# Ending a unit's attention one iteration later instead of four in the first 17 units, and lifting the FFN ration in the last four

## The chip, the cores and the metric

One core of one Trainium2 chip runs the kernel in one launch. The metric is device time in microseconds (us); lower is better. Five engines work side by side, each through its own queue in program order: TensorE (PE in the profile; PEld is its weight load), VectorE (DVE), ScalarE (ACT), GpSimd (POOL) and SyncE (SP, which issues most DMAs).

## The reference

Two stages, all in float32. First an attention that keeps, for every query, only the 32 largest scores of a row; then a gated feed-forward block (SwiGLU) on its output.

```python
scores = scale * np.matmul(q, k.transpose(0, 1, 3, 2))        # 8 batches, 8 heads, 576 x 576
kth = np.partition(scores, -32, axis=-1)[..., -32:-31]
scores = np.where(scores >= kth, scores, -1e9)
attn = softmax(scores)                                         # over the last axis
x = (attn @ v)  -> (B, H, S, D) to (B*S, H*D) = (4608, 512)
g = x @ w_gate                                                 # w_gate, w_val: 512 x 1536
out = (g * sigmoid(g) * (x @ w_val)) @ w_out                   # w_out: 1536 x 512
```

## The kernel before

**Units.** The attention is cut into 160 units: per batch (8), per query tile `qt` of 128 rows (0 to 3, and a rest of 64 rows as `qt` 4), per pair of heads (4). In a unit with `qt` 0 to 3 the two heads lie side by side, 1152 score columns on 128 partitions. With `qt` 4 the two heads' 64 rows share the partitions, so the unit has one head's width (`nh` = 1) and half the work on VectorE. Units 16 to 19 are the first of that kind.

A unit goes through these steps, each on its engine:

- `scores` (L220): four matmuls on TensorE (L250; L236 in a `qt` 4 unit), copied from PSUM to `sc` by ScalarE (L255, L241).
- `select` (L258): the top-k on VectorE, four rounds of `max` (L271) with three of `match_replace` (L275) between, 14 steps for two heads, then a penalty for what lies under the 32nd value (L281).
- `penalize` (L285): GpSimd adds penalty and scores (L293).
- `weigh` (L296): ScalarE's exponential with the row sum (L302).
- `normalize` (L308): GpSimd adds a small constant to the sum (L312), VectorE takes the reciprocal (L314), ScalarE scales (L317).
- `turn` (L319): nine transposes on TensorE (L329), copied out by ScalarE (L330).
- `values` (L340): the product with v on TensorE (L349, L358), copied by ScalarE into a column block `xT` of the FFN's input (L373). `finish_unit` (L507) calls it.

**FFN.** It works on 18 blocks of 256 rows. A block can start when `values` has been issued for all its rows and all four head pairs. The generator `feed` (L398) issues a block in 36 pieces: 24 of four 256-column matmuls (L412; gate and value products by turns, two pieces each) and 12 of two 512-column matmuls with `w_out` (L449). After a gate product ScalarE runs three instructions (L430 to L432) and GpSimd multiplies (L433); after a value product ScalarE copies (L437) and GpSimd multiplies (L438). These follow-ups are queued in `on_act` and `on_pool` and issued where the code calls `flush`, or in `piece` (L471) when more than one waits.

**Weights.** Each of the 72 parts of the FFN weights is loaded and rounded by a chain (`rounded`, L92): a DMA, two ScalarE instructions (L101, L106), GpSimd (L103), VectorE (L110), GpSimd (L113), VectorE (L116). `weights` staggers these, so that a rounding step issues L116, L110 with L113, L101 with L103 and L106, and a DMA, each for another part. Steps are spread between the top-k steps of `dve` (L532), 5 for every 11. Before it issues a matmul, `feed` calls `need` (L147), which issues as many rounding steps at once as are still missing.

**Order.** One loop (L524) writes out the order: iteration n holds the top-k of unit n, the scores of unit n+1, `penalize` and `weigh` of unit n-1, and in between the steps that end older units. The first half of `normalize` (L312) and what follows is for unit n-2, `turn` for n-3 (`TURN`), `values` for n-4 (`VALUES`). At the end of the function every engine is bound to this order, so an engine runs its instructions strictly as written.

**Ration.** `credit` grows by 4.6 in an iteration with two heads and 2.3 with one, to at most 8; a piece costs 1 (`pieces`, L498). It is not raised after unit 159. What is left at the end of the loop is issued without a ration (L576).

Of the kernel before, what the change touches and what calls it, by code (L numbers as in the profile page):

```python
# [27 lines left out]
def kernel(  # L28
# [33 lines left out]
    NHP = H // 2  # L62
# [80 lines left out]
    def rounding(n):  # L143
        for _ in range(n):
            next(weight, None)
# [28 lines left out]
    def load_v(i):  # L174
        b, hp = pairs[i]
        h = slice(2 * hp, 2 * hp + 2)
        vt = slabs.tile([P, 2, J, D], FP32, tag="v", name="v")
        v_last = slabs.tile([R, 2, D], FP32, tag="vl", name="v_last")
        vl = vlast[i % NV]
        nc.sync.dma_start(  # L180
            vt[:].rearrange("p h j d -> p h (j d)"),
            v[b, h, 0:JP].rearrange("h (p j) d -> p h (j d)", j=J),
        )
        nc.sync.dma_start(v_last[:], v[b, h, JP:S].rearrange("h p d -> p h d"))
        for hh in range(2):
            o = hh * R
            nc.sync.dma_start(vl[o : o + R, o : o + R], v[b, 2 * hp + hh, JP:S])
        vs[i] = (vt, v_last, vl)
# [27 lines left out]
    def n_heads(qt):  # L216

        return 1 if qt == J else 2
# [39 lines left out]
    def select(n):  # L258

        nh = n_heads(units[n][1])  # L260
        sc = state[n]["sc"]
        m = small.tile([P, 2, TOP_K], FP32, tag="m", name="m", bufs=2)
        heads = [slice(t * S, (t + 1) * S) for t in range(nh)]
        rest = work.tile([P, 2 * S], FP32, tag="rest", name="rest", bufs=1)
        e = work.tile([P, 2 * S], FP32, tag="e", name="e", bufs=4)
        state[n] |= dict(m=m, e=e, heads=heads)
        cur = sc
        rounds = TOP_K // 8
        for r in range(rounds):
            for t, hs in enumerate(heads):  # L270
                nc.vector.max(m[:, t, 8 * r : 8 * r + 8], cur[:, hs])  # L271
                yield
            if r < rounds - 1:
                for t, hs in enumerate(heads):
                    nc.vector.match_replace(  # L275
                        rest[:, hs], m[:, t, 8 * r : 8 * r + 8], cur[:, hs], LOWEST
                    )
                    yield
                cur = rest
        for t, hs in enumerate(heads):  # L280
            nc.vector.tensor_scalar(  # L281
                e[:, hs], sc[:, hs], m[:, t, TOP_K - 1 : TOP_K], FAR, ALU.is_lt, ALU.mult
            )
# [24 lines left out]
    def normalize(n):  # L308
        st = state[n]
        tot, e, heads = st.pop("tot"), st["e"], st.pop("heads")  # L310
        nh = len(heads)
        nc.gpsimd.tensor_scalar_add(tot[:, 0:nh], tot[:, 0:nh], EPS)  # L312
        yield
        nc.vector.reciprocal(tot[:, 0:nh], tot[:, 0:nh])  # L314
        yield
        for t, hs in enumerate(heads):
            nc.scalar.mul(e[:, hs], e[:, hs], tot[:, t : t + 1])  # L317

    def turn(n):  # L319

        last = units[n][1] == J
        e = state[n].pop("e")
        et = work.tile([P, 2 * J + 1, P], FP32, tag="et", name="et")
        for c0, cn in ((0, J), (J, 1)) if last else ((0, J), (J, 1), (J + 1, J)):
            ps = ps_t.tile([P, 512], FP32, tag="t", name="etps")
            kl = R if last and c0 == J else P
            for c in range(cn):
                k0 = (c0 + c) * P
                nc.tensor.transpose(ps[0:kl, c * P : (c + 1) * P], e[:, k0 : k0 + kl], ident[:])  # L329
            nc.scalar.copy(  # L330
                et[0:kl, c0 : c0 + cn, :],
                ps[0:kl, 0 : cn * P].rearrange("p (c j) -> p c j", c=cn),
            )
            if c0 == J:
                yield
        state[n]["et"] = et
# [3 lines left out]
    def values(n):  # L340

        b, qt, hp = units[n]
        vt, v_last, vl = vs[b * NHP + hp]
        et = state.pop(n)["et"]
        last = qt == J
        ql = R if last else P
        av = ps_t.tile([P, P], FP32, tag="t", name="av")
        if not last:
            nc.tensor.matmul(av[:], vl[:], et[:, J, :], start=True, stop=False)  # L349
        for c in range(J + 1 if last else J):  # L350
            kl = R if c == J else P
            for hh in range(2):
                moving = (
                    et[0:kl, c, hh * R : (hh + 1) * R]
                    if last
                    else et[:, c + hh * (J + 1), :]
                )
                nc.tensor.matmul(  # L358
                    av[hh * R : (hh + 1) * R, 0:ql],
                    v_last[:, hh, :] if c == J else vt[:, hh, c, :],  # L360
                    moving,
                    start=last and c == 0,
                    stop=c == (J if last else J - 1),
                )
        c0 = b * S + qt * P
        at = c0
        while at < c0 + ql:
            kb = at // BLK
            n_c = min((kb + 1) * BLK, c0 + ql) - at
            if kb not in xT:  # L370
                xT[kb] = ffn.tile([P, NHP, BLK], FP32, tag="xT", name="xT", bufs=3)
                done[kb] = 0
            nc.scalar.copy(  # L373
                xT[kb][:, hp, at - kb * BLK : at - kb * BLK + n_c],
                av[:, at - c0 : at - c0 + n_c],
            )
            done[kb] += n_c
            at += n_c
# [88 lines left out]
    NU = len(units)  # L467
# [3 lines left out]
    def piece():  # L471

        if len(on_act) > 1:
            flush(on_act)
        if len(on_pool) > 1:
            flush(on_pool)
        while True:
            if not current:
                if not todo or done.get(todo[0], 0) < NHP * BLK:
                    return False  # L480
                flush(on_act)
                flush(on_pool)
                current.append(feed(todo.pop(0)))
            if next(current[0], 0) == 0:
                current.pop()
                continue
            return True

    def fetch(n):

        b, qt, hp = units[n]
        i = b * NHP + hp
        if qt == 0:
            yield from prep(i)
        if qt == J and i + NHP < len(pairs):
            load(i + NHP)

    def pieces(n):  # L498
        for _ in range(n):
            if credit[0] >= 1 and piece():  # L500
                credit[0] -= 1

    def run(steps):
        for _ in steps:
            pass

    def finish_unit(n):  # L507
        values(n)
        b, qt, hp = units[n]
        if qt == J and b + 1 < B:  # L510
            load_v((b + 1) * NHP + hp)
# [7 lines left out]
    credit = [0.0]  # L519
    no = iter(())  # L520
    over = {}
    TURN, VALUES = 3, 4
    due = [0.0]
    for n in range(NU + VALUES):  # L524
        nh = n_heads(units[n][1]) if n < NU else 1
        topk = select(n) if n < NU else no
        over[n - 1] = normalize(n - 1) if 0 <= n - 1 < NU else no
        nxt = scores(n + 1) if n + 1 < NU else no
        ahead = fetch(n + 2) if n + 2 < NU else no
        norm = over.pop(n - 2, no)  # L530

        def dve(k, beside=True):  # L532

            for _ in range(k * nh):
                next(topk, None)
                due[0] += 5 / 11 if beside else 0
                if due[0] >= 1:
                    due[0] -= 1
                    rounding(1)

        if n < NU:
            credit[0] = min(credit[0] + (4.6 if nh == 2 else 2.3), 8.0)
        flush(on_act)
        next(norm, None)
        if 0 <= n - 1 < NU:
            penalize(n - 1)
        flush(on_pool)
        if 0 <= n - TURN < NU:
            run(turn(n - TURN))
        if n >= VALUES:  # L550
            finish_unit(n - VALUES)
        next(nxt, None)
        if 0 <= n - 1 < NU:
            weigh(n - 1)
        run(nxt)

        dve(2, beside=False)
        if 2 <= n + 2 < NHP:
            load(n + 2)
        if n < NHP:  # L560
            load_v(n)
        pieces(2)
        flush(on_act)
        flush(on_pool)
        dve(2)
        next(norm, None)
        run(norm)
        next(ahead, None)
        pieces(1)
        next(ahead, None)  # L570
        dve(1)
        pieces(1)
        dve(2)
        run(topk)
        pieces(6)
    while piece():  # L576
# [49 lines left out]
```

## Time and profile before

| | |
|---|---|
| time, median of 3 runs | 1922.34 us (1921.83 to 1926.45) |
| the profiled execution | 1924.16 us, span 1922.4 us |
| TensorE busy | 1759.7 us (92%) |
| VectorE busy | 1608.6 us (84%) |
| ScalarE busy | 1156.6 us (60%) |
| GpSimd busy | 815.5 us (42%) |
| mean granted TensorE clock | 0.958 |

The span is the time of one execution between its first and last recorded instruction. Busy shares are means over stages that have different limits, so the stages are to be read one by one. A row of a timeline gives start, duration, engine, line, operation, output and inputs, and in brackets the idle time before it with the instruction that ended it. The first top-k instruction of unit n starts at 138.05 us for n = 9, 166.72 for 11, 252.95 for 16, 281.55 for 20, 334.97 for 25 and 403.40 for 31.

### The profile page before, as it was taken

The page shows a single profiled execution, that of the slowest core. Times are in us where ns is not written, and L with a number is a line of the kernel's source. Part 1 is how long each engine was busy: PE and PEld are TensorE (multiplying, and loading weights), DVE is VectorE, ACT ScalarE, POOL GpSimd, SP SyncE. Part 2 cuts the span into 40 slices and gives each one's busy share as a digit, 9 for nine tenths or more (in the row PEclk, how much of TensorE's full clock was granted, in tenths as well). Part 3 has the DMA queues.
Part 4 walks back from the last instruction along what each step waited for, and adds up shares of the span by engine and source line. Part 5 has one row for each costly group of instructions (what it writes and reads, how often), then busy time and mean ns, then how long its engine had stood idle before and what let it go on. Part 6 is the DMA issues. An engine that isn't in the chain of part 4 may idle for free.

```text
span 1922.4 us, 29365 instructions
## 1 busy us (share of the span) xinstructions
PE 1759.7 (92%) x10144; PEld 1299.6 (68%) x10144; DVE 1608.6 (84%) x3476; ACT 1156.6 (60%) x2821; POOL 815.5 (42%) x846
## 2 busy tenths in 40 slices
PE   3437789989999999999999999999999999999899
PEld 2326558677777777676767776767676767686666
DVE  7999889998899979997899979998899979997300
ACT  5666666566666666665666666666666656665411
POOL 4556634434354434343434343435253525353222
PEclk7668899989999999999999999999999999999899
DMA  7222212000300011000210002000200011000000
GB/s 186 88 80 77 66 27 63 11 2 2 81 7 12 7 35 49 12 6 8 58 30 1 12 16 73 1 12 2 67 22 12 1 27 38 12 1 12 1 11 11
DMA packets 111253, 59.58 MB, mean 31 GB/s; under 512 B 89088, under 2 KB 97280, under 8 KB 111104
## 3 DMA queue, kind: packets, MB, share of 16 engines
q1 hardware_dynamic: 109904, 57.41, 11.3%
q8 instruction: 80, 1.31, 0.3%
q14 instruction: 69, 0.57, 0.1%
q10 hardware_dynamic: 1200, 0.30, 0.1%
HBM read 48.23 MB, written 9.44 MB: 30 GB/s over the span
## 4 chain that ended last, share of the span: by engine, by line
PE 82%; DVE 6%; POOL 5%; ACT 5%; issue 2%; DMA 0%; SPq 0%; POOLq 0%; DVEq 0%; ACTq 0%
PE f L412 38%; PE o_ps L449 19%; PE av L358 7%; PE etps L329 7%; PE s L250 6%; DVE m L271 3%; POOL e L293 2%; DVE rest L275 2%; PE s L236 2%; PE av L349 1%; ACT e L302 1%; PE kqps L205 1%; ACT sc L255 1%; POOL size L113 1%; POOL size L103 1%
## 5 line engine op out<-in xcount | busy, mean ns | idle before, releaser
L271 DVE MAX8 m<-rest 128x8 f32<-128x576 f32 x864 | 615.3, 747 | 2.2
L275 DVE MATCH_REPLACE8 rest<-m,rest 128x576 f32<-128x576 f32 x576 | 424.2, 743 | 0.0
L412 PE MATMUL f<-xT,wg 128*128 128x256 f32 x1728 | 407.5, 386 | 0.0
L293 POOL TENSOR_TENSOR e<-e,sc 128x1152 f32<-128x1152 f32 (+1 forms) x160 | 382.6, 2391 | 44.4 <-DVE e L281 38.4
L412 PE MATMUL f<-xT,wv 128*128 128x256 f32 x1728 | 397.3, 382 | 0.0
L449 PE MATMUL o_ps<-wo,h 128*128 128x512 f32 x864 | 387.2, 598 | 0.0
L412 PEld LDWEIGHTS f<-xT,wg 128*128 128x128 f32 x1728 | 323.9, 191 | 71.7 <-issue 30.4
L412 PEld LDWEIGHTS f<-xT,wv 128*128 128x128 f32 x1728 | 326.3, 191 | 54.4 <-issue 11.3
L433 POOL TENSOR_TENSOR h<-h,half_g 128x512 f32<-128x512 f32 x108 | 138.4, 1281 | 473.3 <-ACT h L432 455.3
L329 PE MATMUL etps<-ident,e 128*128 128x128 f32 (+1 forms) x1312 | 188.4, 288 | 130.9 <-POOL size L103 46.3
L271 DVE MAX8 m<-sc 128x8 f32<-128x576 f32 x288 | 205.6, 751 | 120.7 <-ACT sc L255 77.9
L449 PEld LDWEIGHTS o_ps<-wo,h 128*128 128x128 f32 x864 | 159.6, 190 | 192.9 <-issue 186.8
L329 PEld LDWEIGHTS etps<-ident,e 128*128 128x128 f32 (+1 forms) x1312 | 159.1, 147 | 181.6 <-issue 54.7
L330 ACT COPY et<-etps 128x512 f32<-128x512 f32 (+1 forms) x448 | 184.9, 481 | 147.4 <-PE etps L329 145.8
L302 ACT ACTIVATE e<-e,bias 128x576 f32<-128x576 f32 x288 | 222.0, 776 | 73.9 <-POOL e L293 73.5
L317 ACT ACTIVATE e<-e,tot 128x576 f32<-128x576 f32 x288 | 210.4, 780 | 5.4 <-DVE tot L314 5.1
L275 DVE MATCH_REPLACE8 rest<-m,sc 128x576 f32<-128x576 f32 x288 | 211.9, 742 | 0.0
L438 POOL TENSOR_TENSOR h<-h,val 128x512 f32<-128x512 f32 x108 | 139.6, 1292 | 161.3 <-ACT val L437 161.3
L250 PE MATMUL s<-kqT 64*128 64x288 f32 x1024 | 174.4, 449 | 10.2 <-ACT kqT L210 6.4
L358 PE MATMUL av<-et,v 128*64 128x128 f32 (+1 forms) x2560 | 175.2, 283 | 0.0
L255 ACT COPY sc<-s 128x288 f32<-128x288 f32 x512 | 165.0, 410 | 2.5 <-PE s L250 2.5
L312 POOL TENSOR_SCALAR tot<-tot 128x2 f32<-128x2 f32 (+1 forms) x160 | 37.0, 231 | 305.2 <-ACT e L302 296.5
(44 smaller groups left out, 1436.5 us busy)
## 6 DMA issues: line engine op xcount, KB each, us to landing
kq_in<-in_k_dram SPq DMA_DIRECT2D x64, 128.0 KB, 2.8
v<-in_v_dram SPq DMA_DIRECT2D x32, 256.0 KB, 3.0
kq_in<-in_q_dram SPq DMA_DIRECT2D x62, 128.0 KB, 2.9
w<-in_moe_w_gate_dram SPq DMA_DIRECT2D x24, 256.0 KB, 2.7
w<-in_moe_w_val_dram SPq DMA_DIRECT2D x24, 256.0 KB, 2.7
w<-in_moe_w_out_dram SPq DMA_DIRECT2D x24, 256.0 KB, 2.5
out_dram<-o SPq DMA_DIRECT2D x40, 128.0 KB, 2.4
out_dram<-o SPq DMA_DIRECT2D x16, 256.0 KB, 2.3
```

The source lines that it names most:

```text
L250: nc.tensor.matmul(ps[:, 0:half], slab[d, q0 : q0 + P], slab[d, k0 : k0 + half])
L255: nc.scalar.copy(sc[:, i * half : (i + 1) * half], ps[:, 0:half])
L271: nc.vector.max(m[:, t, 8 * r : 8 * r + 8], cur[:, hs])
L275: nc.vector.match_replace(rest[:, hs], m[:, t, 8 * r : 8 * r + 8], cur[:, hs], LOWEST)
L293: nc.gpsimd.tensor_tensor(e[:, every], e[:, every], sc[:, every], ALU.add)
L302: nc.scalar.activation(e[:, hs], e[:, hs], AF.Exp, bias=bias[:, t : t + 1], scale=scale, accum_out=tot[:, t : t + 1],)
L317: nc.scalar.mul(e[:, hs], e[:, hs], tot[:, t : t + 1])
L329: nc.tensor.transpose(ps[0:kl, c * P : (c + 1) * P], e[:, k0 : k0 + kl], ident[:])
L330: nc.scalar.copy(et[0:kl, c0 : c0 + cn, :], ps[0:kl, 0 : cn * P].rearrange("p (c j) -> p c j", c=cn),)
L358: nc.tensor.matmul(av[hh * R : (hh + 1) * R, 0:ql], v_last[:, hh, :] if c == J else vt[:, hh, c, :], moving, start=last and c == 0, stop=c ...
L412: nc.tensor.matmul(ps[:, i, :], w[:, kc, m * P : (m + 1) * P], x[:, kc, :], start=(kc == 0), stop=(kc == KC - 1),)
L449: nc.tensor.matmul(ps[:], hs[m // 2][:, m % 2, t * P : (t + 1) * P], wo[:, m, :], start=(m == 0), stop=(m == MC - 1),)
```

## The change

Iterations 0 to 16 (`head`) end a unit sooner: the whole of `normalize`, `turn` and `values` for unit n-1 are issued in iteration n, in the course of its top-k steps, instead of in iterations n+1 to n+3. From iteration 17 on the order is as before, and iterations 17 to 19 issue no `values` (17 and 18 no `turn`), since these units are done. The ration in the head is the same as elsewhere. From iteration 156 on the credit is set to 8 in every iteration, which also holds in the four iterations after the last unit.

```diff
+    HEAD = 4 * NHP + 1
     TURN, VALUES = 3, 4
     due = [0.0]
     for n in range(NU + VALUES):
+        head = n < HEAD
...
-        norm = over.pop(n - 2, no)
+        norm = over.pop(n - 1 if head else n - 2, no)
...
-        if n < NU:
+        if n >= NU - NHP:
+            credit[0] = 8.0
+        else:
             credit[0] = min(credit[0] + (4.6 if nh == 2 else 2.3), 8.0)
         flush(on_act)
-        next(norm, None)
+        if not head:
+            next(norm, None)
         if 0 <= n - 1 < NU:
             penalize(n - 1)
         flush(on_pool)
-        if 0 <= n - TURN < NU:
+        if HEAD - 1 <= n - TURN < NU:
             run(turn(n - TURN))
-        if n >= VALUES:
+        if n - VALUES >= HEAD - 1:
             finish_unit(n - VALUES)
...
         pieces(2)
         flush(on_act)
         flush(on_pool)
-        dve(2)
+        dve(1)
+        if head:
+            next(norm, None)
+        dve(1)
         next(norm, None)
         run(norm)
         next(ahead, None)
         pieces(1)
         next(ahead, None)
         dve(1)
         pieces(1)
+        if head and n >= 1:
+            run(turn(n - 1))
         dve(2)
+        if head and n >= 1:
+            pieces(1)
+            finish_unit(n - 1)
         run(topk)
         pieces(6)
```

## The prediction

> **What bounds the kernel now.** I read the page's slices first, then the busy time of each engine by stage, then the VectorE, ScalarE, GpSimd and TensorE timelines around the FFN's start and at the end. Times are us from the span's start. T(n), the start of iteration n, is the start of unit n's first L271 `m<-sc` on VectorE. A piece is one step of `feed`; an iteration issues what the loop body of the same n issues. "About what a measurement of this kernel can tell from no change" is 0.3%, 5.8 us.
>
> The stages (span; PE, PEld, DVE, ACT, POOL busy; PE clock) are units 11 to 15, 16 to 19, 20 to 30, 31 to 155, and the end:
>
> ```profile
> 166.72:252.95 86.23, 72.85 (x379) 56.95 (x376) 71.18 (x160) 53.79 (x132) 54.17 (x70) 0.92 0.17 55
> 252.95:281.50 28.55, 25.30 (x144) 14.01 (x141) 24.62 (x50) 16.13 (x41) 10.39 (x14) 1.00 0.11 30
> 281.50:403.40 121.90, 113.75 (x684) 83.81 (x684) 116.79 (x254) 78.44 (x194) 47.77 (x45) 0.95 0.13 33
> 403.40:1764.20 1360.80, 1337.17 (x7906) 989.42 (x7903) 1223.34 (x2612) 860.63 (x2092) 570.69 (x541) 1.00 0.09 22
> 1764.20:1922.40 158.20, 144.21 (x680) 104.28 (x678) 24.78 (x51) 49.00 (x103) 41.16 (x40) 0.95 0.03 7
> ```
>
> From unit 31 on TensorE is the bound (1337 of 1361 us). Up to unit 31 VectorE sets the pace: 117 of 122 us in units 20 to 30, where a two-head unit takes 10.57 us undisturbed. Before unit 16 it also rounds weights, about 4.5 steps (L116 and L110, 0.6 us together) per unit, and a unit takes 14.1 us. In units 11 to 15, the first with FFN work, it is idle 15 us of 86, for this reason (VectorE, then GpSimd):
>
> ```profile
> 177.16 0.29 DVE L110 TENSOR_SCALAR size<-size 128x256 int32<-128x256 int32 x1 [3.22 <-POOL size L103]
> 174.67 1.28 POOL L433 TENSOR_TENSOR h<-h,half_g 128x512 f32<-128x512 f32 x1 [4.42 <-ACT h L432]
> 194.26 0.72 POOL L113 TENSOR_TENSOR size<-size,ulps 128x256 int32<-128x256 int32 x1
> 195.06 0.40 POOL L103 TENSOR_SCALAR size<-size 128x256 f32<-128x256 f32 x1
> 195.94 0.72 POOL L113 TENSOR_TENSOR size<-size,ulps 128x256 int32<-128x256 int32 x1 [0.48 <-DVE tot L314]
> ```
>
> The queues are in order. The rounding's L103 stands on GpSimd behind an FFN product L433, that waits for ScalarE, that waits for TensorE, and VectorE waits for L103. Where VectorE has nothing else between, one rounding step follows the other after 1.68 us (194.26 to 195.94).
>
> **What moves in number.** By the code's credits (8 at most, 4.6 or 2.3 a unit) FFN block 0 has its input in iteration 8 instead of 11, block 1 in 16 instead of 19. Block 2 needs units 16 to 27, that end late in both, so it starts in iteration 31 in both. Counted through the loop, both kernels have issued 72 pieces by then and hold 8 credits; from there to iteration 155 the order is the same. So the early start wins no FFN work on TensorE: what counts is T(31), 403.4 now, and it carries over in full to the TensorE-bound stretch.
>
> **The head, iteration by iteration.** Now `normalize`'s L312 (GpSimd) stands at the start of an iteration, for a unit one older; afterwards it stands mid-iteration behind one rounding step, for unit n-1, and the reciprocal L314 on VectorE waits for it the same iteration. Queued behind L314 are the remaining 6 to 8 top-k steps and every rounding step. `turn` and `values` follow on TensorE, their PSUM copies on ScalarE.
>
> Iterations 1 to 8, no FFN: after T, L293 ends at 3.0, the exponentials at 4.7, the score copies at 5.7, L103 at 6.7, L312 at 7.0. VectorE comes to L314 between 6.1 and 7.0 (172.81-166.72 unstalled, 159.61-152.62 with its L103 wait). Cost 0.3 each, 2.4 (0 to 6); T(9) = 138.1+2.4 = 140.5.
>
> Iteration 9: six pieces are issued at the end of 8, behind `values(7)`, at T(8)+14 (transposes end at 10.1, copies at 10.9, av 2.6, xT copy 0.4). A piece is 1.72 (20.60 us for twelve at 1835.21; 3.45 for two), so they end at T(9)+10.5. GpSimd's L433 and L438 of these stand ahead of `penalize(8)`, and ScalarE's second gate (L430 to L432, 1.5 us) ahead of unit 8's exponentials. So exponentials end at 14.1, score copies at 15.3, the next value copy (two pieces later) at 16.5, L438 at 17.8, L113, L103 and L312 at 19.2. VectorE arrives at 6.8 and waits some 12 us, on L103 or L312; 7.1 us of work are left, and a cold restart of TensorE can add 1.9 (a piece took 3.78 for 1.89 at 220.06). I take 27.5 (24 to 30).
>
> Iterations 10 to 12: a gate's L433 ends at 8.9, L103 at 10.0, L312 at 10.3; VectorE arrives at 6 to 7. Lengths 17.3, 16.4, 17.3, together 51 (48 to 56); units 11 to 15 now take 16.3, 19.8, 16.3, 18.0, 15.9.
>
> Iteration 13: pieces 27 to 30 ask for the last of `w_out`, so some twelve rounding steps are issued, six and three of them with no top-k between. Each such step takes 1.68 on the L113-L103-L110 circle, VectorE being busy 0.6: 9 x 1.1 idle, plus 2 for the first, behind the score copies. 10.6 + 12 x 0.6 + 9.9 + 2 = 29.7; I take 29.2 (24 to 33). Iterations 14 and 15 have no rounding left: 10.7 each, 21.4 (21 to 24). T(16) = 140.5+27.5+51+29.2+21.4 = 269.6, now 253.0: +16.6.
>
> A rule and a row on the burst. L116 took 2.45 us at 186.44, not 0.41, ending 0.3 us after a GpSimd L293. The Trainium skill ("SBUF — State Buffer", Who interferes with whom) says that a VectorE instruction with two SBUF inputs and a GpSimd one that reads SBUF lock each other out for the whole instruction, and L116 has two. By it each burst step could lose another 0.41, so an estimate for the nine is 3.7 us more; by the 1.68 us row, none. The sum goes by the row.
>
> Iterations 16 to 19: block 1 becomes ready in 16, again with six pieces at the end of the iteration, and `scores(18)` stands behind them on TensorE. After T(16): scale at 6.7, av at 10.3, pieces 10.7 to 21.1, scores at 22.2, a gate (1.5) and exponential (0.9) ahead of the copies, which end at 24.2. VectorE is through units 16 and 17 at 14.5 and waits 10 us. Units 18, 19 and the wait for unit 20's scores: T(20) = T(16)+38 (33 to 41), now 28.6: +9.4. Units 20 to 24: as now, 53.4 (53 to 57). Units 25 to 30 carry no FFN now, as 28 to 30 before: 63.4+1 (63.4 to 68.4), now 68.4: -4. T(31) = 269.6+38+53.4+64.4 = 425.4, +22.
>
> **The end.** Here TensorE waits for a VectorE-GpSimd-ScalarE chain with its FFN pieces held back by credit:
>
> ```profile
> 1782.41 1.38 PE L329 MATMUL etps<-ident,e 128*128 128x128 f32 x9 [2.40 <-issue]
> 1791.20 1.38 PE L329 MATMUL etps<-ident,e 128*128 128x128 f32 x9 [1.40 <-issue]
> 1800.95 0.87 PE L329 MATMUL etps<-ident,e 128*128 128x128 f32 x5 [2.35 <-ACT e L317]
> 1813.80 0.77 PE L329 MATMUL etps<-ident,e 128*128 128x128 f32 x5 [2.46 <-ACT e L317]
> 1816.58 1.33 PE L329 MATMUL etps<-ident,e 128*128 128x128 f32 x5 [0.99 <-ACT e L317]
> 1820.76 3.78 PE L412 MATMUL f<-xT,wg 128*128 128x256 f32 x8
> ```
>
> From 1758.92 TensorE has 72 pieces left, 72 x 1.72 = 123.9, and attention: three units at 3.44 (1772.84 to 1776.28), one at 2.0, then 4.8 and 1.1, 18.2 in all. That is 142.1; it takes 159.1 (to 1918.0). 17 us are waits and the slow clock after them. Without rationing, iterations 156 to 158 issue 8 pieces each and 159 four, TensorE runs on to about 1833, and VectorE's chain (unit 159 scored near 1812, scaled by 1825) is done before it. What stays is the last chain, `turn(159)`, copy, `values(159)`, xT copy, with no piece to cover it, block 17 needing unit 159: 4.5 with its cold piece, taken from 1813.8 to 1822. Gain 12.5 (9 to 15). If the pieces stalled on ScalarE or GpSimd that cover would go; at 1758.92 eight ran in 13.9 us without a wait.
>
> **Sum.** +22-12.5 = +9.5 on the profiled 1924.16 (span 1922.4, 1.8 around it): 1933.7. The median lies 1.8 below that execution, so 1931.8, say 1932.
>
> **Rivals.** *The end decides, faster:* if the six late pieces do not hold up VectorE (holes of 12 and 10 us, in 9 and 16) and little else is lost, the head is near zero and 12.5 stay: 1910 to 1916. For it: TensorE idles 9.1, 7.3 and 7.4 us before L329 at 133.0, 146.8 and 160.7, so there is room for early pieces. Against: the in-order queues of ScalarE and GpSimd. It decides once the head loses under 6.7 us; 0.16.
>
> *The two halves cancel:* one of the three holes (9, 13, 16) is half as deep and the end gives its full 15: head 7 to 18, time 1917 to 1928; 0.22. *The early start changes nothing by count* holds for pieces (72 in both), and is part of all cases.
>
> *The burst and the lock cost more:* rounding circles of 2.1 us, and units 20 to 24 at their upper bound: head 30 to 36, 1940 to 1946; 0.15. The forecast's own case has 0.47, range 1928 to 1940.
>
> **How the numbers follow.** Slower by over 5.8 (above 1928.1): the forecast's case and the burst's, 0.47 + 0.15 = 0.62; same 0.22; faster 0.16. The terms' bounds, taken as independent (root of the squares), give 9 below and 10 above in the head and 3 at the end. From 1916 to 1945 the range takes in all cases but the faster one, 0.16, and the last microsecond of the burst's.
>
> **What would show it.** VectorE waiting over 10 us in iteration 9 on L103 or L312; nine L110 with waits near 1.1 in 13; an `m<-sc` wait near 10 us at unit 18 for L241; T(31) near 425; TensorE without waits from then-155's pieces to the last chain, span from T(156) 12.5 us shorter. T(31) under 410 would make the prediction wrong, as would an end as long as now.

## The result, and the profile after

The changed kernel takes 1934.60 us (median of 4 runs, 1934.09 to 1934.88), the kernel before 1922.19 us on the same chip (median of 4 runs, 1921.83 to 1926.45). The ratio is 1.0058, with a 95% interval of 1.0043 to 1.0073: 0.6% slower. The profiled execution took 1934.38 us with a span of 1932.6, 10.2 more than the span of before. The medians lie 12.4 apart, but the kernel before scatters more than the changed one: in the larger sets of runs beside the experiments its median was 1924.61 us (21 runs) and 1924.25 us (17 runs). The forecast was 1932.0, range 1916 to 1945, slower. One of the four runs of the experiment e9_act below went at a granted TensorE clock of 0.635 and took 3116.72 us, and the time given for it is that of the other three.

The 17 iterations of the head end 16 units early, units 0 to 15; unit 16 is ended as before.

The table by stage of the kernel after, cut at the starts of units 9, 11, 16, 20, 31 and 156 (span; PE, PEld, DVE, ACT, POOL busy with counts; PE clock, DMA share, GB/s):

```profile
139.38:183.17 43.79, 39.49 (x208) 32.58 (x209) 27.48 (x67) 26.09 (x64) 26.93 (x33) 0.96 0.18 57
183.17:268.01 84.84, 63.92 (x279) 36.27 (x277) 69.06 (x161) 47.42 (x119) 46.74 (x63) 0.82 0.19 62
268.01:306.80 38.79, 33.47 (x175) 26.39 (x172) 24.18 (x49) 18.50 (x45) 14.37 (x15) 0.91 0.08 18
306.80:424.52 117.72, 95.72 (x577) 69.83 (x577) 116.62 (x253) 72.57 (x182) 42.14 (x42) 0.88 0.12 30
424.52:1785.32 1360.80, 1337.20 (x7907) 989.39 (x7904) 1223.53 (x2612) 859.91 (x2092) 569.21 (x541) 1.00 0.09 22
1785.32:1932.60 147.28, 140.19 (x680) 102.32 (x678) 24.91 (x51) 48.35 (x103) 41.00 (x40) 0.97 0.03 8
```

Units 31 to 155 take 1360.80 us in both kernels, to the hundredth, with the same TensorE work. So the head is handed over in full, and the whole change stands in two numbers: T(31) is 424.52 instead of 403.40 (+21.1), and the end takes 147.28 instead of 158.20 (-10.9). In iterations 9 and 10 VectorE is busy for 27.5 of 43.8 us. Iterations 16 to 19 take 38.8 us for 24.2 of VectorE work, where before they took 28.6 for 24.6.

The VectorE timeline of after has the stalls of iterations 9, 10, 13 and 18 (in brackets the idle time, and what ended it):

```profile
158.10 0.29 DVE L110 TENSOR_SCALAR size<-size 128x256 int32<-128x256 int32 x1 [12.95 <-POOL size L103]
175.66 0.29 DVE L110 TENSOR_SCALAR size<-size 128x256 int32<-128x256 int32 x1 [3.25 <-POOL size L103]
...
225.51 0.29 DVE L110 TENSOR_SCALAR size<-size 128x256 int32<-128x256 int32 x1 [0.98 <-POOL size L103]
227.11 0.29 DVE L110 TENSOR_SCALAR size<-size 128x256 int32<-128x256 int32 x1 [0.98 <-POOL size L103]
...
292.90 0.76 DVE L271 MAX8 m<-sc 128x8 f32<-128x576 f32 x1 [10.68 <-POOL h L433]
```

Why VectorE stood for 12.95 us is read from GpSimd's timeline up to the same moment:

```profile
144.85 1.42 POOL L433 TENSOR_TENSOR h<-h,half_g 128x512 f32<-128x512 f32 x1 [6.33 <-ACT h L432]
147.35 1.26 POOL L438 TENSOR_TENSOR h<-h,val 128x512 f32<-128x512 f32 x1 [1.08 <-ACT val L437]
148.68 0.22 POOL L291 TENSOR_SCALAR bias<-m 128x2 f32<-128x2 f32 x1
148.86 2.62 POOL L293 TENSOR_TENSOR e<-e,sc 128x1152 f32<-128x1152 f32 x1
151.76 1.27 POOL L433 TENSOR_TENSOR h<-h,half_g 128x512 f32<-128x512 f32 x1 [0.27 <-ACT h L432]
155.63 1.28 POOL L438 TENSOR_TENSOR h<-h,val 128x512 f32<-128x512 f32 x1 [2.60 <-ACT val L437]
156.85 0.73 POOL L113 TENSOR_TENSOR size<-size,ulps 128x256 int32<-128x256 int32 x1
157.67 0.40 POOL L103 TENSOR_SCALAR size<-size 128x256 f32<-128x256 f32 x1
```

GpSimd takes its instructions in the order in which they were issued. Four products of the first FFN pieces stand ahead of the rounding step that VectorE waits for, and `penalize` (L293) stands between them. VectorE stands from 145.15 on; in this time GpSimd works for most of it and waits some 4.0 us (1.08, 0.27, 2.60) for ScalarE, which waits for the pieces on TensorE.

The wait of 10.68 at unit 18 is put down to L433, which L271 doesn't read. L271 reads `sc`, and the chain that leads to `sc` runs over TensorE and ScalarE: six late pieces (the three rows of L412), then the scores of unit 18, then, behind a gate and an exponential, the copy into `sc`:

```profile
278.66 4.25 PE L412 MATMUL f<-xT,wg 128*128 128x256 f32 x16
282.75 3.62 PE L412 MATMUL f<-xT,wv 128*128 128x256 f32 x16
286.20 3.62 PE L412 MATMUL f<-xT,wg 128*128 128x256 f32 x16
289.75 1.19 PE L236 MATMUL s<-kqT 64*64 64x288 f32 x8
...
292.11 0.69 ACT L241 COPY sc<-s 128x288 f32<-128x288 f32 x2
```

At the end TensorE, over the whole of iterations 156 to 159 and what follows, has two waits left. The clock granted to it was 0.50 from 1860.14 to 1866.97 and 1.00 in the stretch up to there, so the pieces behind the waits start slowly:

```profile
1858.13 0.77 PE L329 MATMUL etps<-ident,e 128*128 128x128 f32 x5 [1.74 <-ACT e L317]
1860.76 1.33 PE L329 MATMUL etps<-ident,e 128*128 128x128 f32 x5 [0.99 <-ACT e L317]
...
1864.94 4.70 PE L412 MATMUL f<-xT,wg 128*128 128x256 f32 x16
```

### The profile page after: what moved, and what is told of

It is laid out like the page before. It is cut to its first block, busy times and chain, and to the rows that moved or that the text cites. A ratio compares the mean times of both kernels' runs of the same rounds, so it can differ in the third digit from the quotient of the medians.

```text
span 1932.6 us, 29394 instructions
## 1 busy us (share of the span) xinstructions
PE 1769.6 (92%) x10144; PEld 1302.4 (67%) x10144; DVE 1607.1 (83%) x3476; ACT 1156.2 (60%) x2821; POOL 815.0 (42%) x846
## 4 chain that ended last, share of the span: by engine, by line
PE 81%; DVE 7%; ACT 5%; POOL 4%; issue 3%; DMA 0%; SPq 0%; POOLq 0%; DVEq 0%; ACTq 0%
PE f L412 38%; PE o_ps L449 18%; PE av L358 7%; PE etps L329 7%; PE s L250 6%; DVE m L271 3%; DVE rest L275 3%; POOL e L293 2%; PE s L236 2%; PE av L349 1%; ACT e L302 1%; PE kqps L205 1%; POOL size L113 1%; ACT sc L255 1%; POOL size L103 1%
## 5 line engine op out<-in xcount | busy, mean ns | idle before, releaser
L271 DVE MAX8 m<-rest 128x8 f32<-128x576 f32 x864 | 614.6, 746 | 2.2
L293 POOL TENSOR_TENSOR e<-e,sc 128x1152 f32<-128x1152 f32 (+1 forms) x160 | 382.5, 2391 | 67.0 <-DVE e L281 43.9
L449 PE MATMUL o_ps<-wo,h 128*128 128x512 f32 x864 | 396.6, 608 | 12.1 <-DVE wo L116 12.1
L412 PE MATMUL f<-xT,wg 128*128 128x256 f32 x1728 | 406.3, 385 | 0.0
L412 PE MATMUL f<-xT,wv 128*128 128x256 f32 x1728 | 396.7, 381 | 0.0
L412 PEld LDWEIGHTS f<-xT,wg 128*128 128x128 f32 x1728 | 323.8, 191 | 69.9 <-issue 27.8
L412 PEld LDWEIGHTS f<-xT,wv 128*128 128x128 f32 x1728 | 324.7, 190 | 54.3 <-issue 11.5
L433 POOL TENSOR_TENSOR h<-h,half_g 128x512 f32<-128x512 f32 x108 | 138.4, 1281 | 456.8 <-ACT h L432 438.8
L271 DVE MAX8 m<-sc 128x8 f32<-128x576 f32 x288 | 205.5, 750 | 125.8 <-ACT sc L255 71.3
L302 ACT ACTIVATE e<-e,bias 128x576 f32<-128x576 f32 x288 | 221.9, 776 | 66.2 <-POOL e L293 65.7
L317 ACT ACTIVATE e<-e,tot 128x576 f32<-128x576 f32 x288 | 210.4, 779 | 10.6 <-DVE tot L314 10.2
L438 POOL TENSOR_TENSOR h<-h,val 128x512 f32<-128x512 f32 x108 | 139.4, 1291 | 158.8 <-ACT val L437 158.7
L250 PE MATMUL s<-kqT 64*128 64x288 f32 x1024 | 167.5, 443 | 4.6 <-ACT kqT L210 4.4
L312 POOL TENSOR_SCALAR tot<-tot 128x2 f32<-128x2 f32 (+1 forms) x160 | 36.9, 230 | 318.9 <-ACT e L302 310.6
```

Of the source, the lines that this page charges most:

```text
L250: nc.tensor.matmul(ps[:, 0:half], slab[d, q0 : q0 + P], slab[d, k0 : k0 + half])
L293: nc.gpsimd.tensor_tensor(e[:, every], e[:, every], sc[:, every], ALU.add)
L302: nc.scalar.activation(e[:, hs], e[:, hs], AF.Exp, bias=bias[:, t : t + 1], scale=scale, accum_out=tot[:, t : t + 1],)
L412: nc.tensor.matmul(ps[:, i, :], w[:, kc, m * P : (m + 1) * P], x[:, kc, :], start=(kc == 0), stop=(kc == KC - 1),)
L449: nc.tensor.matmul(ps[:], hs[m // 2][:, m % 2, t * P : (t + 1) * P], wo[:, m, :], start=(m == 0), stop=(m == MC - 1),)
```

## The experiments

The **theory** is that of the prediction: the late pieces of the early FFN blocks stand, with their follow-ups, ahead of `scores`, `penalize` and the rounding chain (holes in 9 and 18); the shortened run-up makes a burst of rounding (13); the end gains by itself. **Rivals:** (a) it is not the pieces but the early end itself, L312 and L314 in the middle of the top-k, that delays VectorE; (b) the two halves act on each other; (c) the burst costs as much as the holes. The starts of units vary between executions: e1_tail issues the same as the kernel before up to iteration 155, yet its T(31) is 2.3 us later, mostly by a wait of 2.17 us ahead of unit 19 that the other execution does not have. Differences of T(31) below that are not read. The end stretch is the time from T(156) to the end of the span. The ratios are to runs of the kernel before on the same chip, each with its 95% interval.

**e1_tail and e2_head: the halves alone.** e1_tail is the kernel before with the new credit at the end; e2_head is the changed kernel with the old credit.

```diff
 e1_tail, against before
-        if n < NU:
+        if n >= NU - NHP:
+            credit[0] = 8.0
+        else:
 e2_head, against after
-        if n >= NU - NHP:
-            credit[0] = 8.0
-        else:
+        if n < NU:
```

> The ration is lifted from iteration 156 on, the head is left as in the kernel before. My theory (the two halves are separate and add): the head keeps T(31) = 403.4, TensorE runs through the end with one last chain of waits; the stretch from T(156) to the end of the span is near the changed kernel's 147.3 instead of 158.2, so the median is 1922.2 - 10.9 = 1911 (1909 to 1913). Rival (the end is shorter only because the head pushes VectorE and TensorE into another phase): 1917 to 1922. Rival (the ration at the end does nothing, TensorE's waits only move): 1922.

> The early end of units 0 to 16 alone, the ration of the end as in the kernel before. My theory: T(31) near 424.5 as in the changed kernel, the end near 158, median 1922.2 + 21 = 1943 (1941 to 1946). Rival (the head's loss is partly given back by 155, so that the two halves do not add): 1930 to 1938.

e1_tail: 1913.69 us (6 runs), ratio 0.9945 (0.9932 to 0.9957), end stretch 147.3. The end is as expected; the time is just above its range, which was counted from 1922.2, and is 10.9 under the 1924.61 of the larger set of before. e2_head: 1944.44 us (4 runs), ratio 1.0106 (1.0093 to 1.0119), T(31) 424.04, end stretch 158.15. Each end stretch is that of the kernel with the same credit to 0.1 us, and T(31) of e2_head is that of the change to 0.5. The halves add; rival (b) falls. (The later runs with a credit of 8 have end stretches of 147.2 to 149.0.)

**e3_late and e4_round: the holes and the burst.** e3_late issues no piece at the close of iterations 8 and 16; e4_round rounds 6 steps for 11 top-k steps instead of 5.

```diff
 e3_late, against after
-        pieces(6)
+        if n not in (8, 16):
+            pieces(6)
 e4_round, against after
-                due[0] += 5 / 11 if beside else 0
+                due[0] += 6 / 11 if beside else 0
```

> The changed kernel without the pieces at the very end of iterations 8 and 16, which are then issued from the next iteration on. My theory (two of the three holes come from these late pieces, that stand ahead of unit 8's and unit 16's chains and of unit 18's scores): VectorE's wait of 12.95 in iteration 9 falls under 4, that of 10.68 at unit 18 under 5, though the pieces that follow later cost some 3 to 5 each; T(31) near 411 (407 to 417), median 1934.6 - 13 = 1921 (1917 to 1927). Rival (the wait of iteration 9 belongs to the early normalize itself, not to the pieces): the 12.95 stays above 9 and the time within 4 of 1934.6.

> The changed kernel with weight rounding spread at 6 steps for 11 top-k steps instead of 5, so that iteration 13 asks for no step in a row. My theory (the third hole is the burst): the run of 0.98 to 1.9 waits on L103 in iteration 13 goes, iteration 13 takes 17 to 20 instead of 30 while iterations 1 to 12 take 0.6 longer each for the work moved there; T(16) near 259 (256 to 264), median 1934.6 - 9 = 1926 (1922 to 1930). Rival (the burst only holds work that has to be done anyway, and the denser rounding waits as long on GpSimd spread out): within 3 of 1934.6.

e3_late: 1927.19 us (10 runs), 1.0009 (1.0000 to 1.0018), T(31) 417.17. Its VectorE timeline, iterations 9 and 10:

```profile
149.70 0.29 DVE L110 TENSOR_SCALAR size<-size 128x256 int32<-128x256 int32 x1 [3.98 <-POOL size L103]
172.53 0.29 DVE L110 TENSOR_SCALAR size<-size 128x256 int32<-128x256 int32 x1 [6.61 <-POOL size L103]
```

The wait of 12.95 is down to 3.98 and the one at unit 18 is gone, so the late pieces made both. But iteration 10 now waits 6.61 instead of 3.25, and the burst moved to iteration 14 (22.5 us). T(31) gained 7.4 us where 13 were expected, and the time lies just above the expected range: the six pieces come later, and cost there.

e4_round: 1928.20 us (8 runs), 1.0020 (1.0011 to 1.0030), T(31) 416.75. Iteration 13 takes 12.3 us instead of 30.0; 9.2 of that gain are paid back as T(9) is 148.6 instead of 139.4, for the added steps run with the top-k of units 1 to 8. That is 1.15 us an iteration where 0.6 was expected, but iteration 13 also became shorter than expected, and the time lies in the expected range. Spreading the burst is thus worth about 8 us net; rival (c) is right in that holes and burst are alike in size.

**e7_both: the two together.**

> The changed kernel with both edits of e3_late and e4_round: no pieces at the end of iterations 8 and 16, rounding at 6 for 11. My theory: the burst is gone and the waits of 9 and 18 are small, but pieces that follow at the end of 9 and in 17 still cost as in e3_late; T(31) near 413 (409 to 416), median 1924 (1920 to 1927), still 10 above the tail alone. Rival (the holes were all of the loss): T(31) near 403 and median 1913.

1927.36 us (10 runs, 1918.70 to 1929.43), 1.0001 (0.9986 to 1.0015), T(31) 415.09. T(31) is as expected, the time just above its range. The two cures do not add (7.4 and 7.8 of T(31) alone, 9.4 together). What is left shows in its trace as waits of 3.64, 6.62, 4.18 and 4.11 us on L103 in iterations 9 to 12, in which the early FFN pieces run.

**e5_wait: the early end without early FFN.** `piece` starts block 0 in iteration 11 and block 1 in 19 at the earliest, as the kernel before did; all else is the change.

```diff
+                if n < {0: 11, 1: 19}.get(todo[0], 0):
+                    return False
                 flush(on_act)
```

> The changed kernel, early end of units included, but FFN block 0 may not start before iteration 11 nor block 1 before 19, as in the kernel before. My theory (the early end alone costs VectorE 0.2 to 0.3 an iteration, and the loss comes from FFN pieces that start early and late in their iteration): T(11) near 168, waits of 3 to 7 in 11 to 15 (three pieces still stand at the end of 11), no run of waits on L103 in iteration 13, no wait near 10 at unit 18; T(31) near 410 (405 to 413) instead of 424.5, median near 1924.6 + 7 - 10.9 = 1920.5 (1916 to 1924). Rival (the loss belongs to the early normalize, turn and values, whatever the FFN does): T(31) above 418, median above 1928.

1912.36 us (4 runs), 0.9935 (0.9922 to 0.9949), T(31) 401.99, both 8 us below the expectation and outside its range. Units 11 to 15, 16 to 19 and 20 to 30 of this kernel, in the columns of the stages above:

```profile
168.20:256.03 87.83, 71.59 (x351) 55.05 (x351) 71.11 (x159) 53.07 (x130) 54.25 (x69) 0.88 0.18 55
256.03:282.66 26.63, 26.42 (x127) 13.46 (x127) 24.52 (x50) 14.94 (x37) 10.05 (x13) 1.00 0.14 36
282.66:401.99 119.33, 112.00 (x682) 83.63 (x680) 116.44 (x255) 77.35 (x192) 48.14 (x45) 0.95 0.12 32
```

The burst doesn't come (FFN starts when it used to), nor do the holes, and units 16 to 30 are 4.5 us shorter than before: VectorE's waits for score copies (2.90, 0.53, 1.72, 1.33 and 1.49 before units 20 to 30) are down to 1.32 and 1.50. A likely cause is that no `turn` and `values` are left for iterations 17 and 18; that was not tried by itself. So rival (a) falls: T(31) is 1.4 us under that of before and 3.7 under e1_tail's, so ending a unit early costs nothing on balance. The loss in the head, 22.5 us of T(31) against the changed kernel, belongs to the FFN work that it lets in early.

**e6_pool: GpSimd's follow-up behind the rounding step.** In e1_tail the waits on L103 in units 11 to 15 are 3.21, 2.88, 2.68, 3.47 and 2.79, 15.0 in all, and the prediction had laid them to an L433 ahead of L103. Here GpSimd's follow-ups are issued behind it:

```diff
         flush(on_act)
-        flush(on_pool)
+        if n > 4 * NHP:
+            flush(on_pool)
         dve(2)
+        flush(on_pool)
```

> The kernel before with the ration lifted at the end (as e1_tail), and in iterations 0 to 16 the GpSimd follow-ups of the FFN (L433, L438) issued behind the rounding steps of the next four top-k steps instead of ahead of them. My theory (what costs in iterations 11 to 15 is L433 standing ahead of L103): the five waits of L110 on L103, 3.2, 2.9, 2.7, 3.5 and 2.8, shrink to under 1 each, T(16) near 241 instead of 252.7, T(31) near 393, median 1913.7 - 11 = 1903 (1899 to 1908). Rival (the wait only moves to the next rounding step, that now stands behind the same product): within 4 of 1913.7.

1911.89 us (6 runs), 0.9928 (0.9916 to 0.9940); T(16) 249.07, T(31) 401.86. A miss: the time is only 1.8 us under that of e1_tail, inside the 4 us that were named for the rival, and the intervals of the two ratios overlap. The waits shrank to 1.59, 1.17, 1.03, 1.83 and 1.15, 6.8 in all, not to under 1 each. Of these 8.2 us less, 4.4 came through: units 11 to 15 take 81.8 us instead of 86.2, for VectorE is busy for 75.0 us in them instead of 71.1. GpSimd's and VectorE's timelines in iterations 11 and 12 show both what is left of the waits and something new:

```profile
175.66 0.40 POOL L103 TENSOR_SCALAR size<-size 128x256 f32<-128x256 f32 x1 [2.06 <-ACT size L101]
176.03 1.27 POOL L433 TENSOR_TENSOR h<-h,half_g 128x512 f32<-128x512 f32 x1
```

```profile
176.10 1.35 DVE L110 TENSOR_SCALAR size<-size 128x256 int32<-128x256 int32 x1 [1.59 <-POOL size L103]
193.79 0.29 DVE L110 TENSOR_SCALAR size<-size 128x256 int32<-128x256 int32 x1 [1.17 <-POOL size L103]
```

L103 now waits for ScalarE's L101, which stands behind the gate (L430 to L432, to 175.2) on ScalarE. And L110 takes 1.35 instead of 0.29, beside the L433 that was moved there: part of the wait came back as longer VectorE instructions.

**e8_six, e9_act and e10_best: what that points to.** e8_six is e6_pool with 6.0 for 8.0 as the credit of the end, so that pieces are left for the last chain. e9_act moves ScalarE's follow-ups behind the same point as GpSimd's. e10_best is e5_wait with the credit of 6.0 and both follow-ups behind `normalize` in the head. e11_act_again is e9_act once more, for its trace.

```diff
 e8_six, against e6_pool
-            credit[0] = 8.0
+            credit[0] = 6.0
 e9_act, against e8_six
-        flush(on_act)
         if n > 4 * NHP:
+            flush(on_act)
             flush(on_pool)
         dve(2)
+        flush(on_act)
         flush(on_pool)
 e10_best, against e5_wait, beside credit 6.0
-        flush(on_act)
-        flush(on_pool)
+        if not head:
+            flush(on_act)
+            flush(on_pool)
...
         run(norm)
+        if head:
+            flush(on_act)
+            flush(on_pool)
```

> As e6_pool, with the credit set to 6 instead of 8 from iteration 156 on, so that four pieces are left to stand between the last units' chains in iteration 160. My theory (the changed kernel's last waits, 1.7 and 1.0 on L317 with a slow piece after them, are there because no piece was left): the stretch from T(156) to the end 2 to 4 shorter than 147.3, median 2 to 4 under e6_pool. Rival (the last chain is not covered because block 17 needs it whatever stands before): equal to e6_pool within 1.

> As e8_six, with ScalarE's FFN follow-ups of iterations 0 to 16 (the gate, L430 to L432) issued behind the next four top-k steps as well, so that they stand behind the rounding's L101 of these steps. My theory (what e6_pool left of the five waits of L110 in iterations 11 to 15, 1.2 to 1.8 each, is L101 and so L103 behind the gate): they fall under 1.0, that sum of 6.7 to under 4, T(31) near 398 instead of 401.9, median 1906.7 - 3.5 = 1903 (1900 to 1906). Rival (it is TensorE's lateness, not ScalarE's order): waits unchanged, within 1.5 of 1906.7.

> The early end of units as in e5_wait (FFN blocks 0 and 1 not before iterations 11 and 19), the credit of 6 from iteration 156 on, and in the head both kinds of FFN follow-ups issued behind normalize and two rounding steps. My theory (the early end is harmless, the FFN's follow-ups ahead of the chain cost): the waits of 11 to 15 on L103 or L312, 16.2 in all in e5_wait, fall to under 8, T(31) near 392 (387 to 398) instead of 402, the end near 143; median 1912.4 - 10 - 4.4 = 1898 (1893 to 1904). Rival (normalize in the same iteration keeps VectorE waiting whatever stands before it): T(31) above 399, median above 1905.

> The kernel of e9_act once more, for its trace. My theory: the five waits of L110 in iterations 11 to 15 together under 4 (e8_six: 6.8), T(31) near 396, about 1901. Rival (the gain of 6 lies elsewhere, in the end or in units 16 to 30): waits near 6.8 and T(16) near 249.

e8_six: 1906.66 us (4 runs), 0.9901 (0.9888 to 0.9915), end stretch 142.8, 4.5 less, a little over the expected 2 to 4. Its TensorE has one wait left in the end, and no slow piece behind it (4.70 above); its granted clock was 1.00 throughout the end stretch:

```profile
1836.30 0.76 PE L329 MATMUL etps<-ident,e 128*128 128x128 f32 x5 [0.99 <-ACT e L317]
...
1838.75 3.72 PE L412 MATMUL f<-xT,wg 128*128 128x256 f32 x16
```

e9_act: 1900.4 us (3 runs), 0.9869 (0.9852 to 0.9885). e11_act_again: 1902.05 us in one run; T(16) 244.64, T(31) 396.66. Its waits on L103 from iteration 11 on are 0.29, 0.99, 0.29, 0.99 and 0.62, 3.2 in all, two of them in iteration 11. The longer one there:

```profile
178.93 0.29 DVE L110 TENSOR_SCALAR size<-size 128x256 int32<-128x256 int32 x1 [0.99 <-POOL size L103]
```

So of the 15.0 us that VectorE waited on L103 in units 11 to 15, 8.2 went with GpSimd's order and 3.6 with ScalarE's, and 3.2 are left.

e10_best: 1900.13 us (4 runs), 0.9867 (0.9851 to 0.9884); T(31) is 395.43, and the waits on L103 and L312 in iterations 11 to 15 sum to 8.5, a little over the 8 that was expected.

Both beat both kernels by over 1%, but not by the order of follow-ups alone. Against the span of before, e11_act_again is 22.1 us shorter: 15.4 of this is the end (142.8 instead of 158.2, from the credit) and 6.7 is T(31). For e10_best it is 23.2, some 15 and 8. The early end is not needed for it: e9_act does without and is as fast.

## Why the prediction was right

The sum was +22 - 12.5 = +9.5 on the profiled execution, and +10.2 came. By its steps (us):

| step | predicted | measured |
|---|---|---|
| iterations 1 to 8 | +2.4 | +1.5 (114.49 from T(1) to T(9), 113.01 before) |
| iteration 9, its wait | 27.5, some 12 | 26.54, 12.95 |
| iterations 10 to 12 | 51 | 51.0 |
| iteration 13 | 29.2 | 29.97 |
| iterations 14, 15 | 21.4 | 21.1 |
| iterations 16 to 19, wait at unit 18 | 38, 10 | 38.8, 10.68 |
| units 20 to 24; 25 to 30 | 53.4; 64.4 | 53.2; 64.6 |
| T(31) | 425.4 | 424.52 |
| end | -12.5 | -10.9 |

**By count nothing is won.** The equal middle stretch shows that 72 pieces in both by iteration 31 mean no less work for TensorE. e5_wait adds that the early end by itself costs nothing up to T(31); the 0.2 us an iteration that it takes in iterations 1 to 8 (0.3 was charged) comes back later.

**The burst** is a circle, as said: 1.61 us a step, with VectorE waiting 0.98 of it (1.68 was used, from one pair of rows). Five steps wait 0.98 and two 1.87 and 1.53, where nine near 1.1 were forecast. That iteration 13 came out within 0.3 us of the 29.7 that were counted is luck in part: VectorE waited 9.6 us in it where 11.9 were counted, and was busy for 20.4 where 17.8 were. The lock that the prediction weighed and left out costs next to nothing in the circle: at 225.71 L116 takes 0.42, and GpSimd's next L113, which starts 0.24 later, at 225.95, takes 0.76 (0.72 at 230.77, with no L116 beside it). Outside the circle it does cost, see below; one L110 of 1.36 us fell into iteration 13, at 220.34.

**The end** was mis-sized: waits and slow clock cost 6.0, not 4.5 (TensorE runs from 1780.03 to 1928.1, 148.1 us for 142.1 of work). The step that failed is "unit 159 scaled by 1825", before TensorE has used up its pieces. That is 61 us after T(156); in the changed kernel it happened 75 us after, and the pieces that TensorE had at hand had ended at 70. ScalarE, GpSimd and VectorE at that place:

```profile
1855.00 0.58 ACT L460 COPY o<-o_ps 128x512 f32<-128x512 f32 x1 [5.36 <-PE o_ps L449]
...
1856.54 0.78 ACT L302 ACTIVATE e<-e,bias 128x576 f32<-128x576 f32 x1
```

```profile
1857.50 0.21 POOL L312 TENSOR_SCALAR tot<-tot 128x1 f32<-128x1 f32 x1 [6.57 <-ACT e L302]
```

```profile
1857.74 0.16 DVE L314 RECIPROCAL tot<-tot 128x1 f32<-128x1 f32 x1 [8.27 <-POOL tot L312]
```

With the credit at 8, ScalarE stands in front of the copy of an FFN output (L460) that TensorE has not finished, and unit 159's exponential (L302, at 1856.54) is queued behind it, and behind that unit 158's L317 (1857.31), for which TensorE waits 1.74 us. The prediction had the pieces as cover and put a stall of theirs on ScalarE at nothing, from eight that ran without a wait at 1758.92; here such a stall makes the chain late. With a credit of 6 (e8_six) unit 159's L314 runs 65.6 us after T(156) instead of 72.4, but its L317 stands behind such a copy again and runs at 72.8 instead of 74.6. TensorE waits 0.99 instead of 2.73, its clock stays at 1.00, and 4.5 us of the end come back. Whether they come from the earlier chain or from the pieces that now stand between the last units' chains was not tried apart.

**What was incomplete** is the reading of before's 3 us waits as "L103 stands behind L433". It is about half of it: L103's own input L101 stands behind the gate on ScalarE (e6_pool against e11_act_again). The forecast did not depend on it, since both follow-ups were left in place. The rival in which the two halves cancel was mis-summed: a head of 7 to 18 us gives 1917 to 1928 with the 12.5 of the forecast, and with the full 15 of the end that the rival names, 1914 to 1925. That T(31) would fall by 13 when the late pieces are held back, and that the early end would cost some microseconds, were the two expectations after it that missed (e3_late, e5_wait), beside that of e6_pool.

## What to carry to other kernels

Before an early start is credited, count the work of the bound engine up to the point from which the order is the same; if it is equal, only the stalls on the way are left, and they can be counted from the queues. A piece of work let in early brings its follow-ups on every in-order queue, and these, as well as the piece, can hold up the next unit's chain: issue a follow-up behind the short steps that another engine waits for, on each engine it passes, and look at what it then runs beside. At the end of this kernel a ration that was loosened took 10.9 us off, and one that kept some pieces for the last chains 4.5 more; other values than 8 and 6 were not tried.

## What the runs showed of the hardware that was not expected

In these traces a short VectorE instruction that starts under a GpSimd product stands, in nearly every case, until that is done. The rows are those that start between 60 and 260 us in ten traces (all but e2_head, e7_both and e9_act). L110 took 0.28 to 0.30 us in all 543 cases in which no GpSimd instruction was running as it started. Where an L433 or L438 was running, 14 of 16 took 1.35 to 1.37 and ended 0.15 or 0.16 us after the product (176.10 + 1.35 = 177.45 above, the product at 177.30); in the other two L110 kept its 0.28, and the product took 1.67 and 1.54 us instead of 1.27. L116 took 0.40 to 0.42 in all 469 cases with no GpSimd instruction running, and 0.63 to 1.47 in the 43 that started under those products. The Trainium skill ("SBUF — State Buffer", Who interferes with whom) says that an instruction with two SBUF inputs, as L116, is locked out by a GpSimd one that reads SBUF, and that `tensor_scalar`, as L110, can be too when it runs in a two-port mode; the rows agree with both. No run here shows which mode L110 ran in.
